# Score and value-query products of a recurrent attention as pairs of 64-row array tiles

## The chip, the cores and the metric

The kernel runs on one core of a Trainium2 chip. The metric is the device time of one execution in microseconds (us). The core has five engines with queues of their own: TensorE (PE, with its weight loads listed as PEld), VectorE (DVE), ScalarE (ACT), GpSimd (POOL) and SyncE (SP), which starts most of the transfers. An engine runs its queue in order and waits on semaphores for the others. PE writes its results to PSUM, which has eight banks of 128 partitions by 512 float32 words; DVE and ACT bring them back to the main on-chip memory.

## The reference

Three stages follow each other. The attention is a recurrence over 768 tokens for 4 batches of 8 heads with 40 dimensions; its output is the input of a mixture of 8 experts, and that of one a two-layer network.

```python
for t in range(S):
    y[:, :, t] = np.einsum('bhd,bhde->bhe', rt, state)
    Sa = np.einsum('bhde,bhe->bhd', state, at)
    state_decay = state * wt[:, :, None, :] - np.einsum('bhd,bhe->bhde', Sa, bt)
    state = state_decay + np.einsum('bhd,bhe->bhde', vt, kt)
...
logits = x @ w_gate                      # x: the attention's output, 3072 x 320
expert_idx = np.argmax(logits, axis=1)   # each token to one expert, in order, up to its capacity
h = np.maximum(np.einsum('ecd,edf->ecf', disp, w1), 0.0)
y = np.einsum('ecf,efd->ecd', h, w2)     # times the gate, back to the tokens' rows
...
h = x @ w_in
g = np.where(h > 0.0, h, alpha * (np.exp(np.minimum(h, 0.0)) - 1.0))
return (g @ w_out).astype(np.float32)
```

## The kernel before

**Units.** The attention is done in chunks of 64 tokens. A unit is one chunk of half the batches, 16 matrices for 16 pairs of batch and head; there are 24 units (12 chunks, two halves each), and a chunk needs the state that the chunk before it left. The 40 dimensions of a head lie on 64 partitions, two heads (called hp or x, 0 and 1) on partitions 0 to 63 and 64 to 127, so that most tiles are 128 partitions high with 8 groups (called q) along the row.

**Steps.** Each step is a generator, and each yield ends a part. `pre_dve(u)` (p) forms the running products of the decays by two scans on DVE (L220, L225), multiplies a by one (L230) and k and b by the other (L232). `pre_act(u)` (a) copies the scaled a on ACT into block-diagonal form (L241, tile `Abd`, off-diagonal blocks zero) and once more next to the masked scores (L243, tile `AM`). `scores(u, g)` (c) multiplies k and b against a for four of the eight groups (L254, tile `sc`); ACT copies the lower half of the result for the triangular inverses (L258), and `am_evac` (m) masks the upper half on DVE (L272). `q_mm(u, g)` (q) multiplies the solved values against the queries (L502, tile `q`, moving operand `Rbd`, block-diagonal as well) and masks the result on DVE (L507). Around them stand `kb_tr` (k, L281 and L283), `t64` (g, L410 and L421, preceded by a transpose on DVE, L403), `u_solve` (u, L446), `vu_tr` (w, L456), `s_update` (s, L471 on PE, L480 to L485 behind it), `s_tr` (h, L493), `y_state` and `y_mm` (z and y, L516 and L529, then L533 on DVE), `rhs` (r, L436) and `x_out` (x, L539, then L544 on ACT and L546 on DVE). GpSimd solves the triangles for four units at a time (L328, L330).

**Order.** The order of issue on every engine is fixed by the program: a table, `ORDER`, for the first five slots, and `slot(k)` for each later slot k. Slot k finishes unit k, and computes the scores of unit k + 8 and the scans of unit k + 9, as long as there are such units. In a slot from k = 5 to 15 the string that `slot` returns reads, in part (c.0 and c.1 stand for the score steps of unit k + 8, q.0 and q.1 for the value-query steps of unit k - 1; several marks of one name are its parts):

```
r r c.0 g g m.0 c.0 x x x g g (i) c.1 m.1 c.1 c.1 l q.0 q.0 u u q.1 q.1 h h (b) k.0 k.0 k.1 k.1 e p p p g w w w w a a z d t s s s y y
```

Slots 16 to 24 have the same without c, m, l, k, e, p and a. PSUM is one pool of seven banks that are handed out in turn (`bank`), and an eighth for y.

**After the attention** the experts and the second network run as blocks of 512 rows. They begin with rows that the attention has scattered to device memory (`disp`), so their first block can't start before the attention's last units are done.

Of the kernel before, what the change touches and what calls it, by code (L numbers as in the profile page):

```python
# [23 lines left out]
# units whose inverses start from blocks of 16 rows, and those with a plain product for the turn of k and b  # L24
FU, KMU = 4, 8
GROUPS = [(u, 2) for u in range(0, FU, 2)] + [(u, 4) for u in range(FU, NU, 4)]
# parts of the steps (see steps in attention) in the order of issue up to slot KR; slot() gives the later ones
KR = 5
ORDER = """
se1 sa0 se0 se0 v1 sc0 e0.0 sv se1 e0.1 sd p0 sw p0 e1.0 sw a0 p0 v0 p1 sa1 sx a0 p1 lw sz v2 st2 ss2 st1 e2.0 c0.0 a1  # L30
# [68 lines left out]
def attention(tc, nc, e_in, v_tok, d_in, wg, disp, cst, ring, early):  # L99
# [11 lines left out]
    # tiles that the first weights take over when the loads and scores are done  # L111
# [19 lines left out]
    Abd = [sh[2][:, 1024 * i:1024 * i + 1024].rearrange("p (x q t) -> p x q t", x=2, t=64) for i in range(2)]  # L131
# [28 lines left out]
    def set_a(i):  # L160
        nc.gpsimd.memset(Abd[i], 0.0)
# [55 lines left out]
    def pre_dve(u):  # L217
        e, s, g, d = EI[u % 2], SE[u % 2], GE[u % NGE], DF
        pc = PC[0:104, u % NPC, :]
        nc.vector.tensor_tensor_scan(  # L220
            out=s[0:104, ::-1], data0=e[0:104, 2:522][:, ::-1], data1=DR[0:104, ::-1],
            initial=0.0, op0=ALU.mult, op1=ALU.add)
        nc.vector.tensor_tensor(pc, s[0:104, 0:520:65], e[0:104, 1:521:65], op=ALU.mult)
        nc.vector.reciprocal(d[0:104, 0:520:65], pc)
        nc.vector.tensor_tensor_scan(  # L225
            out=g[0:104], data0=e[0:104, 0:520], data1=d[0:104],
            initial=0.0, op0=ALU.mult, op1=ALU.add)
        a, kb = Aes[u % 2][0:104].rearrange("p (q t) -> p q t", t=64), KBt[u % 2][0:104]
        yield
        nc.vector.tensor_tensor(a, a, q64(g)[0:104], op=ALU.mult)  # L230
        yield
        nc.vector.tensor_tensor(kb, kb, q64(s)[0:104].unsqueeze(2).to_broadcast([104, 8, 2, 64]), op=ALU.mult)  # L232

    def pre_act(u):
        AM, A = AMs[u % (LOOK + 1)], Abd[u % 2]
        for hp in range(2):
            if hp:
                yield
            r = slice(64 * hp, 64 * hp + 64)
            x = Aes[u % 2][r].rearrange("p (q t) -> p q t", t=64)  # L240
            nc.scalar.copy(A[r, hp], x)  # L241
            if u >= 2:
                nc.scalar.copy(AM[64:128, :, hp, :], x)  # L243

    # 64 x 64 matrices in rows of 4160: their diagonal blocks of 16 start 1040 apart
# [3 lines left out]
    def scores(u, g):  # L249
        A, kb = Abd[u % 2], KBt[u % 2]  # L250
        p = st["sc", u, g] = bank("sc")
        for i in range(4):
            q = 4 * g + i
            nc.tensor.matmul(  # L254
                p[:, 128 * i:128 * i + 128], kb[:, q].rearrange("p x t -> p (x t)"),
                A[:, :, q, :], start=True, stop=True)
        yield
        nc.scalar.copy(AB[64:128, :, 2 * g:2 * g + 2], p[64:128, :].rearrange("p (j b y) -> p b j y", j=2, b=2))  # L258
        if g == 0:
            return  # L260
# [9 lines left out]
    def am_evac(u, g):  # L270
        AM, p = AMs[u % (LOOK + 1)], st["sc", u, g]
        nc.vector.tensor_tensor(  # L272
            AM[0:64, 4 * g:4 * g + 4].rearrange("p q x t -> p (q x) t"), p[0:64, :].rearrange("p (l t) -> p l t", t=64),
# [15 lines left out]
    # inverses of triangles: of 16 rows for the first two pairs of units, of 32 for each four of the others  # L289
# [19 lines left out]
    def solve(g):  # L309
        """the inverse a part of its steps at a time"""  # L310
# [55 lines left out]
    # unit 1 has what a later unit's scores take over  # L366
# [3 lines left out]
    def t32(u):  # L370
        """blocks of 32 rows from those of 16"""
# [27 lines left out]
    def t64(u):  # L399
        """blocks of 64 rows from those of 32"""  # L400
# [86 lines left out]
    def s_tr(u):  # L487
        # for unit u: S0' in d-major
# [8 lines left out]
    def q_mm(u, g):  # L497
        V, R = VUt[u % 2], Rbd[u % 2]
        p = bank("q")
        for i in range(4):  # L500
            h = 4 * g + i
            nc.tensor.matmul(p[:, 128 * i:128 * i + 128], V[:, h].rearrange("p x t -> p (x t)"), R[:, h], start=True, stop=True)  # L502
# [3 lines left out]
        Qs, m = st["Qs", u], mask.unsqueeze(1).to_broadcast([128, 8, 64])  # L506
        nc.vector.tensor_tensor(Qs[:, 4 * g:4 * g + 4].rearrange("p h b t -> p (h b) t"), p.rearrange("p (l t) -> p l t", t=64), m, op=ALU.mult)  # L507
# [44 lines left out]
    def route(u, n=2):  # L552
        """expert of the tokens of n units from u on"""
# [14 lines left out]
    def route_mm(u, n=2):  # L568
        """their rows"""
# [38 lines left out]
    def go(key):  # L608
        """the next part of a step"""
# [31 lines left out]
def consts(p):  # L641
    """tiles that last, unset"""
# [29 lines left out]
def set_rest(nc, c):  # L672
# [3 lines left out]
    t = c["tri"]                          # 1 where k < m  # L676
    g.affine_select(out=t, in_=t, pattern=[[1, 128]], base=0, channel_multiplier=-1, compare_op=ALU.is_gt, fill=0.0)
    t = c["blk"]                          # same half
    g.memset(t[0:64, 64:128], 0.0)
    g.memset(t[64:128, 0:64], 0.0)  # L680
    t = c["tmo"]                          # same half: -1 where k >= m
# [3 lines left out]
    t = c["l1"]                           # first half before second half  # L685
# [11 lines left out]
class Ring:  # L697
    """tiles in turn, each for the weights of four tiles: [tile][three k tiles of stage one | stage two]"""
# [9 lines left out]
class Weights:  # L708
# [8 lines left out]
    def split(s, g):  # L717
        """high and low parts, a tile at a time"""
# [26 lines left out]
def ahead(W):  # L745
    """loads and splits of the first weights, a piece at a time"""
    W.fetch(0)
    yield
    yield from W.split(0)
    W.fetch(1)  # L750


def ffn(tc, nc, cst, disp, cap, w1, w2, w_in, w_out, out, ring, W0):
# [6 lines left out]
    # results: 512 rows of each expert, then a row of every token for those past them  # L760
# [6 lines left out]
    def convert():  # L767
        """float64 bits of the second network's weights to float32, rounded to nearest; a piece at a time"""
# [17 lines left out]
        for i, (g, k) in enumerate(jobs):  # L786
# [14 lines left out]
            # magnitudes below the least normal float32 become zero  # L801
# [9 lines left out]
    class Block:  # L811
        """512 rows through one pair of weights"""
# [17 lines left out]
        def start(s):  # L830
            """load and preparation of a block that nothing hides, a tile of rows at a time"""
# [68 lines left out]
    def elu(p, H, L):  # L900
        # GpSimd has the weights to split in the first block
# [6 lines left out]
        # exp(n) - 1 = (exp(n) + 1) tanh(n / 2), which keeps its digits at small n  # L908
# [5 lines left out]
    def gates():  # L914
        """gate weight of every token, zero where the expert is full"""
# [39 lines left out]
        # row of the result: inside the first 512 of its expert, or the token's own  # L955
# [14 lines left out]
    def run(blocks, extra, back=1):  # L970
        """blocks in turn; side work spread over the stages"""
# [22 lines left out]
    # experts  # L994
# [4 lines left out]
    def experts(r, dyn=False, more=None):  # L999
        Ws = [W0 if not dyn and e == 0 else expert(nc, ring, w1, w2, e) for e in range(8)]  # L1000
        hs = [(W, h) for W in Ws for h in range(2)] + ([] if dyn else [(W2, 0), (W2, 1)])
        def put(Y, i, dst, last):
            # the last rows on their own where the gathers wait for them
# [63 lines left out]
    def overflow():  # L1067
        # rows past the first 512 of an expert
# [24 lines left out]
        with tc.For_i(1, nr, 1) as r:  # L1093
            # zero rows behind the last row in use
# [11 lines left out]
            # this round's results to the tokens' own rows  # L1106
# [37 lines left out]
def host_layout(r, k, v, w, a, b):  # L1144
    def e_side(x):
        # [4, 8, 768, 40] -> [c, B2, hp, e, j, bp, t]
        y = x.reshape(2, 2, 4, 2, 12, 64, 40)          # B2 bp j hp c t e
# [3 lines left out]
    # decays with a zero before each chunk and two behind the last  # L1151
# [5 lines left out]
    y = v.reshape(2, 2, 4, 2, 12, 64, 40)              # B2 bp j hp c t d  # L1157
    v_tok = np.ascontiguousarray(y.transpose(4, 0, 5, 2, 1, 3, 6)).reshape(24, 64, 640)

    def d_side(x):  # L1160
        y = x.reshape(2, 2, 8, 12, 64, 40)             # B2 bp h c t d
# [39 lines left out]
```

## Time and profile before

| | us |
|---|---|
| median of 3 runs (1161.91, 1166.55, 1170.0) | 1166.55 |
| span of the profiled execution, first to last instruction | 1160.2 |
| PE busy in it | 1004.3 |
| DVE busy | 769.6 |
| POOL busy | 615.1 |
| ACT busy | 498.3 |

The profiled execution's span is 1.7 us below the fastest of the three timed runs and 6.35 us below their median. Its time stamps start at the first instruction. A float32 matmul stands in the profile as two records, each with a weight load of its own. The busy time of PE counts a matmul until its modelled end, while the next one has already begun, so starts of neighbouring rows tell more of its pace than lengths do.

### The profile page before, as it was taken

How to read it: one execution, taken by the hardware profiler on the slowest of the kernel's cores; microseconds unless marked ns; L12 is line 12 of the kernel's file. 1: busy time of each engine (PE TensorE's matmuls, PEld its weight loads, DVE VectorE, ACT ScalarE, POOL GpSimd, SP SyncE). 2: the span in 40 equal slices, each digit the busy share in tenths (PEclk: the TensorE clock that was granted, in tenths of full speed). 3: DMA queues.
4: the chain of work that ended last, by engine and by line, in shares of the span. 5: the costliest groups of instructions: out<-in, count | busy, mean ns of one | idle time of the engine just before them, and what ended most of it. 6: DMA issues, size and time to landing. Idle time of an engine off the chain costs nothing. (4 is left out here: it accounts for less than half of the span.)

```text
span 1160.2 us, 25498 instructions
## 1 busy us (share of the span) xinstructions
PE 1004.3 (87%) x10287; PEld 910.5 (78%) x10287; DVE 769.6 (66%) x1234; ACT 498.3 (43%) x968; POOL 615.1 (53%) x699
## 2 busy tenths in 40 slices
PE   5777889888899995788977798969999999999992
PEld 5777888788799894777867687847799999999992
DVE  8767666766765343588977888948666666666652
ACT  4555455545454341232332233325555455545441
POOL 4759577684928522345544545626664545454451
PEclk8878888988889897898988998979999999999997
DMA  6687764667644444425465646413010101010001
GB/s 173 160 177 200 180 139 101 129 167 168 150 116 101 130 116 142 142 80 190 149 179 176 193 131 201 173 57 123 1 46 1 46 1 46 1 46 1 23 1 29
DMA packets 189214, 127.25 MB, mean 110 GB/s; under 512 B 102776, under 2 KB 177016, under 8 KB 187448
## 3 DMA queue, kind: packets, MB, share of 16 engines
q1 hardware_dynamic: 185336, 108.65, 35.8%
q0 software_dynamic: 3168, 11.03, 2.9%
q10 hardware_dynamic: 576, 5.77, 1.3%
q8 instruction: 85, 1.39, 0.5%
q14 instruction: 49, 0.40, 0.1%
HBM read 87.39 MB, written 38.03 MB: 108 GB/s over the span
## 5 line engine op out<-in xcount | busy, mean ns | idle before, releaser
L912 POOL TENSOR_TENSOR L<-E,H 128x512 fp32r<-128x512 f32 x91 | 141.8, 1558 | 162.7 <-ACT H L911 157.4
L885 PE MATMUL po<-ring,L 128*128 128x320 f32 x640 | 200.8, 314 | 14.0 <-DVE L L898 9.9
L883 PE MATMUL po<-ring,H 128*128 128x320 f32 x640 | 199.0, 311 | 1.3 <-ACT H L911 0.8
L723 POOL TENSOR_TENSOR ring<-ring,ring 128x704 fp32r<-128x704 f32 x80 | 147.3, 1853 | 98.1 <-ACT ring L722 83.8
L884 PE MATMUL po<-ring,H 128*128 128x320 f32 x640 | 198.5, 310 | 0.0
L869 PE MATMUL ph<-XH,ring 128*128 128x512 f32 x640 | 185.6, 413 | 4.6 <-DVE XL L860 4.0
L885 PEld LDWEIGHTS po<-ring,L 128*128 128x128 f32 x640 | 121.1, 189 | 18.7 <-DVE L L898 12.4
L869 PEld LDWEIGHTS ph<-XH,ring 128*128 128x128 f32 x640 | 117.6, 196 | 22.7 <-DVE XL L860 5.0
L883 PEld LDWEIGHTS po<-ring,H 128*128 128x128 f32 x640 | 121.5, 190 | 10.5 <-ACT H L911 4.4
L884 PEld LDWEIGHTS po<-ring,H 128*128 128x128 f32 x640 | 121.1, 189 | 6.0
L905 ACT ACTIVATE E<-N 128x512 f32<-128x512 f32 x96 | 60.8, 633 | 150.3 <-POOL L L912 115.6
L904 DVE TENSOR_SCALAR N<-ph 128x512 f32<-128x512 f32 x96 | 66.0, 688 | 74.9 <-PE ph L869 74.7
L330 POOL TENSOR_TENSOR X<-X,ring 128x60 f32<-128x60 f32 (+19 forms) x170 | 105.7, 622 | 13.3
L254 PE MATMUL sc<-ring,ring 128*128 128x128 f32 x384 | 70.5, 346 | 36.9 <-ACT ring L241 25.5
L869 PE MATMUL ph<-XL,ring 128*128 128x512 f32 x320 | 101.8, 400 | 0.0
L869 PE MATMUL ph<-XS,ring 128*128 128x512 f32 x320 | 100.9, 397 | 0.0
L254 PEld LDWEIGHTS sc<-ring,ring 128*128 128x128 f32 x384 | 62.7, 250 | 39.3 <-ACT ring L241 29.6
L328 POOL TENSOR_TENSOR ring<-X,ring 128x60 f32<-128x60 f32 (+19 forms) x108 | 63.4, 587 | 55.9 <-DMA ring<-dab 34.3
L909 DVE SCALAR_TENSOR_TENSOR M<-E,M 128x512 f32<-128x512 f32 x96 | 81.3, 846 | 2.5 <-ACT M L906 2.5
L797 POOL TENSOR_TENSOR M<-M,N 128x320 f32<-128x320 f32 (+1 forms) x28 | 29.5, 1053 | 89.4 <-DVE M L795 89.4
L843 PE MATMUL pt<-ident,X 128*128 128x128 f32 (+1 forms) x168 | 30.8, 314 | 49.9 <-DMA X<-disp 41.4
L869 PEld LDWEIGHTS ph<-XL,ring 128*128 128x128 f32 x320 | 62.3, 195 | 14.7
(212 smaller groups left out, 1997.5 us busy)
## 6 DMA issues: line engine op xcount, KB each, us to landing
ring<-in_w_dram SPq DMA_DIRECT2D x16, 640.0 KB
ring<-in_e_in_dram SPq DMA_DIRECT2D x28, 321.6 KB
ring<-in_w_dram SPq DMA_DIRECT2D x32, 256.0 KB
RVU<-in_d_in_dram SPq DMA_DIRECT2D x48, 160.0 KB
dab<-AB SPq DMA_DIRECT2D x24, 256.0 KB
ring<-w ACTq DMA_DIRECT2D x4, 1408.0 KB
disp<-ring SPq DMA_DIRECT2D x8, 640.0 KB
S<-in_w_out_dram SPq DMA_DIRECT2D x16, 320.0 KB
```

Source lines behind the costliest of these rows:

```text
L254: nc.tensor.matmul(p[:, 128 * i:128 * i + 128], kb[:, q].rearrange("p x t -> p (x t)"), A[:, :, q, :], start=True, stop=True)
L328: nc.gpsimd.tensor_tensor(tv, X[:, 0:n, s:s + 1].to_broadcast([128, n, m]), N[:, s:s + 1, s + 1:e].to_broadcast([128, n, m]), op=ALU.mult)
L330: nc.gpsimd.tensor_tensor(X[:, 0:n, s + 1:e], X[:, 0:n, s + 1:e], tv, op=ALU.subtract)
L723: s.nc.gpsimd.tensor_tensor(s.L[g][:, c], R[:, c], s.H[g][:, c].bitcast(F32), op=ALU.subtract)
L869: nc.tensor.matmul(p, l, r, start=i == 0, stop=i == len(seq) - 1)
L883: nc.tensor.matmul(o, H[:, c], hb, start=f == 0, stop=False)
L884: nc.tensor.matmul(o, H[:, c], lb, start=False, stop=False)
L885: nc.tensor.matmul(o, L[:, c], hb, start=False, stop=last)
L904: nc.vector.tensor_scalar(N, p, 0.0, None, op0=ALU.min)
L905: nc.scalar.activation(out=E, in_=N, func=AF.Exp)
L909: nc.vector.scalar_tensor_tensor(out=M, in0=E, scalar=1.0, in1=M, op0=ALU.add, op1=ALU.mult)
L912: eng.tensor_tensor(L, E, H.bitcast(F32), op=ALU.subtract)
```

## The change

The off-diagonal zeros are no longer multiplied. The two heads of a group, on partitions 0 to 63 and 64 to 127, get a matmul each, with 64 rows of contraction, the same 128 weight columns, and 64 moving columns instead of 128; the first writes to one PSUM bank, the second to another. A group of eight products is now sixteen, and all sixteen are issued by the first part of the first step (c.0, q.0); the second step (c.1, q.1) only evacuates the second bank. Evacuations keep their number and size; their index says which head, no longer which four groups.

`Abd` and its copies on ACT (L241) are gone: DVE writes the scaled a to a tile of its own (`As`, three in turn), from which PE reads directly and ACT makes the copy next to the scores. The zeros that `Abd` needed at the start (two memsets of 128 x 1024 on POOL) become one of 32 x 1536. `Rbd` stays as it is, since `y_state` uses it; `q_mm` takes its diagonal blocks. The rest of the diff strips comments.

```diff
-se1 sa0 se0 se0 v1 sc0 e0.0 sv se1 e0.1 sd p0 sw p0 e1.0 sw a0 p0 v0 p1 sa1 sx a0 p1 lw sz v2 st2 ss2 st1 e2.0 c0.0 a1
+se1 sa se0 se0 v1 sc0 e0.0 sv se1 e0.1 sd p0 sw p0 e1.0 sw a0 p0 v0 p1 sx a0 p1 lw sz v2 st2 ss2 st1 e2.0 c0.0 a1
...
-    Abd = [sh[2][:, 1024 * i:1024 * i + 1024].rearrange("p (x q t) -> p x q t", x=2, t=64) for i in range(2)]
+    As = [sh[2][:, 512 * i:512 * i + 512].rearrange("p (q t) -> p q t", t=64) for i in range(3)]
...
-    def set_a(i):
-        nc.gpsimd.memset(Abd[i], 0.0)
+    def set_a():
+        nc.gpsimd.memset(sh[2][96:128, 0:1536], 0.0)
...
-        nc.vector.tensor_tensor(a, a, q64(g)[0:104], op=ALU.mult)
+        nc.vector.tensor_tensor(As[u % 3][0:104], a, q64(g)[0:104], op=ALU.mult)
...
     def pre_act(u):
-        AM, A = AMs[u % (LOOK + 1)], Abd[u % 2]
+        AM = AMs[u % (LOOK + 1)]
         for hp in range(2):
             if hp:
                 yield
-            r = slice(64 * hp, 64 * hp + 64)
-            x = Aes[u % 2][r].rearrange("p (q t) -> p q t", t=64)
-            nc.scalar.copy(A[r, hp], x)
             if u >= 2:
-                nc.scalar.copy(AM[64:128, :, hp, :], x)
+                nc.scalar.copy(AM[64:128, :, hp, :], As[u % 3][64 * hp:64 * hp + 64])
...
-    def scores(u, g):
-        A, kb = Abd[u % 2], KBt[u % 2]
-        p = st["sc", u, g] = bank("sc")
-        for i in range(4):
-            q = 4 * g + i
-            nc.tensor.matmul(
-                p[:, 128 * i:128 * i + 128], kb[:, q].rearrange("p x t -> p (x t)"),
-                A[:, :, q, :], start=True, stop=True)
-        yield
-        nc.scalar.copy(AB[64:128, :, 2 * g:2 * g + 2], p[64:128, :].rearrange("p (j b y) -> p b j y", j=2, b=2))
-        if g == 0:
+    def scores(u, hp):
+
+        if ("sc", u) not in st:
+            kb, a = KBt[u % 2], As[u % 3]
+            st["sc", u] = P = [bank("sc") for _ in range(2)]
+            for q in range(8):
+                for x in range(2):
+                    r = slice(64 * x, 64 * x + 64)
+                    nc.tensor.matmul(P[x][:, 64 * q:64 * q + 64], kb[r, q].rearrange("p x t -> p (x t)"), a[r, q], start=True, stop=True)
+        yield
+        p = st["sc", u][hp]
+        nc.scalar.copy(AB[64:128, :, :, 64 * hp:64 * hp + 64], p[64:128, :].rearrange("p (j b t) -> p b j t", b=2, t=64))
+        if hp == 0:
             return
...
-    def am_evac(u, g):
-        AM, p = AMs[u % (LOOK + 1)], st["sc", u, g]
+    def am_evac(u, hp):
+        AM, p = AMs[u % (LOOK + 1)], st["sc", u][hp]
         nc.vector.tensor_tensor(
-            AM[0:64, 4 * g:4 * g + 4].rearrange("p q x t -> p (q x) t"), p[0:64, :].rearrange("p (l t) -> p l t", t=64),
+            AM[0:64, :, hp, :], p[0:64, :].rearrange("p (q t) -> p q t", t=64),
             mask[0:64].unsqueeze(1).to_broadcast([64, 8, 64]), op=ALU.mult)
...
-    def q_mm(u, g):
-        V, R = VUt[u % 2], Rbd[u % 2]
-        p = bank("q")
-        for i in range(4):
-            h = 4 * g + i
-            nc.tensor.matmul(p[:, 128 * i:128 * i + 128], V[:, h].rearrange("p x t -> p (x t)"), R[:, h], start=True, stop=True)
+    def q_mm(u, b):
+        if ("q", u) not in st:
+            V, R = VUt[u % 2], Rbd[u % 2]
+            st["q", u] = P = [bank("q") for _ in range(2)]
+            for h in range(8):
+                for bp in range(2):
+                    r = slice(64 * bp, 64 * bp + 64)
+                    nc.tensor.matmul(P[bp][:, 64 * h:64 * h + 64], V[r, h].rearrange("p x t -> p (x t)"), R[r, h, bp], start=True, stop=True)
         yield
...
-        Qs, m = st["Qs", u], mask.unsqueeze(1).to_broadcast([128, 8, 64])
-        nc.vector.tensor_tensor(Qs[:, 4 * g:4 * g + 4].rearrange("p h b t -> p (h b) t"), p.rearrange("p (l t) -> p l t", t=64), m, op=ALU.mult)
+        nc.vector.tensor_tensor(
+            st["Qs", u][:, :, b, :], st["q", u][b].rearrange("p (h t) -> p h t", t=64),
+            mask.unsqueeze(1).to_broadcast([128, 8, 64]), op=ALU.mult)
```

On PE in slot 8, from the last `rhs` to the first `kb_tr`, the kernel before issues these matmuls (a row is the line, the tile written, the operands, the shape of one result and the number of matmuls; `sc` holds scores, `xp` and `t` the two products of `t64`, `q` the value-query products, `ut` those of `u_solve`):

```order
L436 MATMUL rhs<-VS_146,AM_143 64x40 x16
L254 MATMUL sc<-ring_99,ring_97 128x128 x4
L410 MATMUL xp<-AB,TA 32x32 x16
L539 MATMUL x<-IW,XT 128x88 x4
L421 MATMUL t_2882<-TT_129,TA 32x32 x16
L254 MATMUL sc<-ring_99,ring_97 128x128 x4
L502 MATMUL q<-RVU_126 128x128 x4
L446 MATMUL ut<-TT_129,RH_130 64x64 x16
L502 MATMUL q<-RVU_126 128x128 x4
L493 MATMUL s<-ident,S0E_132 128x104 x4
```

In the changed kernel the same place reads:

```order
L435 MATMUL rhs<-VS_146,AM_143 64x40 x16
L254 MATMUL sc<-ring_99,ring_97 128x64 x16
L409 MATMUL xp<-AB,TA 32x32 x16
L541 MATMUL x<-IW,XT 128x88 x4
L420 MATMUL t_3044<-TT_129,TA 32x32 x16
L503 MATMUL q<-RVU_126 128x64 x16
L445 MATMUL ut<-TT_129,RH_130 64x64 x16
L492 MATMUL s<-ident,S0E_132 128x104 x4
```

The second half of the scores has moved ahead of both products of `t64` and of `x`, and the second half of the value-query products ahead of `u_solve`.

On ACT in the same slot, from `vu_tr` to the copy of `x_out`, the kernel before issues (`ring_99` is the shared buffer that holds `Abd`, `ring_98` the one with the loaded operands):

```order
L460 COPY VU<-vu 128x320 x2
L241 COPY ring_99<-ring_98 64x512
L243 COPY AM_143<-ring_98 64x8x64
L241 COPY ring_99<-ring_98 64x512
L243 COPY AM_143<-ring_98 64x8x64
L485 COPY VS_145<-S0E_133 64x8x40
L438 COPY RH_131<-rhs 128x320
L415 COPY TA<-xp 32x256 x2
L258 COPY AB<-sc 64x2x256
L544 COPY XO<-x 128x320
```

And the changed kernel (`ring_99` now holds `As`):

```order
L459 COPY VU<-vu 128x320 x2
L240 COPY AM_143<-ring_99 64x8x64 x2
L484 COPY VS_145<-S0E_133 64x8x40
L437 COPY RH_131<-rhs 128x320
L414 COPY TA<-xp 32x256 x2
L257 COPY AB<-sc 64x8x64
L546 COPY XO<-x 128x320
```

The two copies into `Abd` are gone, and nothing else has moved. DVE issues the same instructions in the same order in both kernels.

## Rows read from the trace of the kernel before

**Rows 1.** Busy time by stretch: length, PE, PEld, DVE, ACT, POOL, PEclk, DMA.

```profile
11.00:151.00 140.00, 113.43 (x1908) 107.63 (x1910) 99.03 (x154) 74.77 (x158) 85.29 (x170) 0.81 0.74 180
151.00:343.00 192.00, 169.77 (x2959) 159.20 (x2956) 129.26 (x229) 95.89 (x210) 131.59 (x201) 0.86 0.59 140
343.00:434.00 91.00, 88.69 (x1925) 83.15 (x1925) 40.87 (x104) 38.04 (x91) 48.09 (x75) 0.94 0.47 111
434.00:1160.20 726.20, 632.41 (x3505) 560.54 (x3501) 492.11 (x720) 285.97 (x501) 340.22 (x227) 0.94 0.28 88
```

**Rows 2.** Waits from 151 to 343 us: total, times, longest.

```profile
DVE Qs L507 <- PE q L502: 23.8, 22, 2.0
...
PE sc L254 <- ACT ring L241: 14.5, 9, 3.5
```

**Rows 3.** Timeline of DVE in slot 8: start, length, instruction, idle before it.

```profile
206.18 1.22 DVE L232 TENSOR_TENSOR ring<-ring 104x1024 f32<-104x1024 f32 x1
...
209.56 0.69 DVE L533 TENSOR_TENSOR XT<-y,GE 104x512 f32<-104x512 f32 x1
...
214.07 0.69 DVE L507 TENSOR_TENSOR Qs<-q,mask 128x512 f32<-128x512 f32 x1 [0.21 <-PE q L502]
216.24 0.69 DVE L507 TENSOR_TENSOR Qs<-q,mask 128x512 f32<-128x512 f32 x1 [1.48 <-PE q L502]
216.85 1.23 DVE L220 TENSOR_TENSOR_SCAN ring<-ring,DR 104x520 f32<-104x520 f32 x1
```

**Rows 4.** Timeline of PE in slot 8.

```profile
208.24 1.16 PE L254 MATMUL sc<-ring,ring 128*128 128x128 f32 x8 [1.53 <-ACT ring L241]
...
210.31 1.12 PE L539 MATMUL x<-IW,XT 128*128 128x88 f32 x8 [0.29 <-DVE XT L533]
211.36 0.69 PE L421 MATMUL t<-TT,TA 32*32 32x32 f32 x32
211.99 1.16 PE L254 MATMUL sc<-ring,ring 128*128 128x128 f32 x8
212.98 1.06 PE L502 MATMUL q<-RVU 128*128 128x128 f32 x8
213.97 1.15 PE L446 MATMUL ut<-TT,RH 64*64 64x64 f32 x32
215.05 1.16 PE L502 MATMUL q<-RVU 128*128 128x128 f32 x8
216.04 0.52 PE L493 MATMUL s<-ident,S0E 104*128 104x104 f32 x4
```

**Rows 5.** Timeline of the weight loads in slot 8 (rows*columns of the weights).

```profile
204.34 1.02 PEld L529 LDWEIGHTS y<-Qs,KB 128*64 128x64 f32 x32
...
210.31 0.97 PEld L539 LDWEIGHTS x<-IW,XT 128*128 128x128 f32 x8 [0.40 <-DVE XT L533]
...
212.87 0.97 PEld L502 LDWEIGHTS q<-RVU 128*128 128x128 f32 x8
213.97 1.01 PEld L446 LDWEIGHTS ut<-TT,RH 64*64 64x64 f32 x32
```

**Rows 6.** Timeline of ACT in slot 8.

```profile
206.30 0.62 ACT L241 COPY ring<-ring 64x512 f32<-64x512 f32 x1 [3.19 <-DVE ring L230]
...
207.57 0.61 ACT L241 COPY ring<-ring 64x512 f32<-64x512 f32 x1
```

**Rows 7.** Groups of the whole span: busy, mean ns, idle before and its releasers.

```profile
L241 ACT COPY ring<-ring 64x512 f32<-64x512 f32 x48 | 29.6, 617 | 46.4 <-DVE ring L230 42.1 <-POOL TOK L692 3.6
```

**Rows 8.** Timeline of PE in slot 10, at the lower clock.

```profile
244.54 2.08 PE L254 MATMUL sc<-ring,ring 128*128 128x128 f32 x8 [3.51 <-ACT ring L241]
```

**Rows 9.** Timeline of DVE in slot 10.

```profile
242.49 1.65 DVE L232 TENSOR_TENSOR ring<-ring 104x1024 f32<-104x1024 f32 x1
...
256.28 0.69 DVE L507 TENSOR_TENSOR Qs<-q,mask 128x512 f32<-128x512 f32 x1 [1.47 <-PE q L502]
```

## The prediction

> **What bounds the kernel now.** I read the busy times by stretch first. The products that change stand before 434 us; from there on the experts and the second network run [rows 1], which the change doesn't touch and which begin with rows that the attention has written. So a microsecond saved before 434 us is one saved at the end, and the question is what sets the pace there. There are three stretches. Up to 151 us the program fills its pipeline (13 score steps, 4 value-query steps), with PE busy 113.43 of 140 us. From 151 to 343 us run slots 5 to 15, eleven slots of 17.5 us, each with one score step and one value-query step; PE is busy 169.77 of 192 us and DVE 129.26. From 343 us no scores are left, and PE is busy 88.69 of 91 us: it is the bound there, back to back.
>
> For the middle stretch, the waits show DVE and PE waiting for each other: the mask of the value-query products (L507) waits 23.8 us for PE, and the scores (L254) 14.5 us for the ACT copies into `Abd` [rows 2]. The timelines of slot 8 show the loop. DVE ends the scaling of k and b at 207.40 [rows 3]; PE starts the scores at 208.24, behind the second `Abd` copy, which ran from 207.57 to 208.18 [rows 4, 6]; `x` begins at 210.31, held by DVE's L533, which ends at 210.25 [rows 3, 4]; then come the second scores, the first q, `u_solve` and the second q at 215.05, and DVE, after its first L507, stands still for 1.48 us until the second [rows 3, 4]. Behind that second L507 the scans of the next unit (L220, 216.85) are queued, and with them the next slot. That is what a change has to shorten.
>
> **The matmuls themselves.** Four products of 128 x 128 by 128 columns take 0.99 us, from 211.99 to the next group at 212.98 and again to 213.97 [rows 4], so a step of eight takes 1.98. What sets this? The eight weight loads of `x` last 0.97 us and those of q last 0.97 too [rows 5], though `x` streams 88 columns and q 128. So the load of 128 weight columns sets the pace, 0.12 us each, and not the moving columns, which are all that the change halves. Per step there are now 32 loads of 128 columns, where there were 16.
>
> Rows matter as little: 32 loads of 64 columns take 1.01 us in `u_solve` with 64 rows and 1.02 in `y_mm` with 128 [rows 5]. The Trainium skill, TensorE: Matmul & The Clock Gate, section LDWEIGHTS, states it as a rule that speaks against this change: a load's time goes by columns, and a load with few rows takes as long as one with all. The rows above agree, though none of them shows a load of 64 rows by 128 columns. By that rule alone, loads one behind the other, a step would take 3.9 us; it is the second case below.
>
> But two array tiles can load at once: 32 loads of 64 columns are 2048 columns in 1.01 us, against 1024 in 0.97 for q [rows 5]. In `u_solve` the two tiles differ in rows and in columns, in `y_mm` in columns alone; no row has tiles that differ in rows alone, as here. So the price of a step lies between 0.97 us (the pair side by side and the 64 moving columns as the measure) and 32 x 0.12 = 3.9 us (no overlap at all). I take the pair side by side with 128 columns as the measure, 16 x 0.12 = 1.94 us, which is nearest to the rows of `u_solve`: PE's time stays as it was. (The Trainium skill, TensorEngine Tiling, section Key Properties, says that different tiles can load and multiply in parallel; the trace agrees for the tiles it has.)
>
> **What moves.** Taking slot 8 with steps of 1.95 us. The scores wait for `As` and for the scaled k and b, so they start at 207.45 instead of 208.24 and end at 209.4; the first half of `t64` takes 0.65 and `x` still waits for L533 until 210.31, so the 0.8 us are lost there. The second `t64` starts at 211.36 as now, and PE goes straight to q at 211.99 and ends it at 213.94. The first L507 starts at 214.1, as now (214.07). The second no longer waits behind `u_solve`: it follows after 0.61, at 214.7, and L220 at 215.3 instead of 216.85. Gain 1.55 us, all of it from closing the gap of 1.48 before the second L507.
>
> In slots at half clock, such as slot 10 (2.08 us for the same eight records [rows 8]), PE is the bound from the scores to q, and its work is the same. There the gain is the earlier start, 244.54 minus the end of L232 at 244.14 [rows 8, 9], 0.4 us, plus the 1.08 of `u_solve` that no longer lie ahead of the second L507 (which waits 1.47 in that slot too [rows 9]), less the 0.61 of the first: 0.87. A mean granted clock of 0.86 [rows 1] between levels of 1 and 0.5 means 28% of the stretch at half clock, 3 slots of 11. Sum for the middle: 8 x 1.55 + 3 x 0.87 = 15.0 us.
>
> Before 151 us: ACT loses 26 of the 48 copies of 0.617 us [rows 7], 16 us, but it is busy 74.77 of 140 us [rows 1], and where PE waited for a copy there, k and b were ready little earlier; between 0 and half of the 16, I take 2. The memsets on POOL (two of 128 x 1024 against one of 32 x 1536) lie beside loads that the first scan waits for: nothing. After 343 us: same loads, same number of mode changes around q (`t64`, q, `u_solve`, `s_tr`), nothing. Two PSUM banks are held at once instead of one after the other; the seven banks go round in about half a slot, and the bank that comes seven allocations after the scores is that of `u_solve`, behind both of their evacuations, so no wait is added. Evacuations move the same number of words with a stride of 64 words inside the row; I count nothing. What hides the longer first score group (1.95 instead of 1.0 us before `t64`) is DVE's work up to L533; without it each slot would lose 0.8.
>
> Sum: 15 + 2 = 17 us off the span of 1160.2, which gives 1143.2. The median of the timed runs is 6.35 us over that span, so 1149.6: **1150 us**.
>
> **The rivals.**
> - *PE gives it back* (no change). If PE is the bound in most of the middle slots, not DVE's chain, closing DVE's gap only lengthens another wait. For it: PE is busy 88% of that stretch. Against: it still waits 14.5 us for the copies and 1.53 us in slot 8 [rows 2, 4]. Gain per slot 0.4 us: 1166.55 - 11 x 0.4 = 1162.
> - *The loads of the two row tiles queue* (slower). A step takes 3.96 instead of 1.98 us. In slot 8: scores to 211.4, `x` 212.05, second `t64` 213.1, q from 213.75 to 217.7, the two masks, L220 at 219.2: 2.35 us later than now. Times 11 slots 26 us; 9 value-query steps after 343 us, where PE has no slack, 18; 17 steps before 151 us at 1.98, about 27 of 34 since PE is busy 81%. Sum 71 minus 2: 1235 us. It decides if the loads of a pair overlap by less than about a fifth. For it: no row shows two loads into the same columns at once. Against: both kinds of pairs that the trace has do overlap.
> - *Half the columns, half the time* (much faster). A step takes 0.97. The slots at half clock, bound by PE, gain about 3 us more each, the last 9 value-query steps 1 each, the 17 early ones half of that: 17 + 9 + 9 + 8.5 = 43, so 1123 us. Against it stand the equal loads of `x` and q. The Trainium skill, TensorEngine Tiling, section Theoretical Speedup, has this rule: up to 2x for a small contraction. The rows on loads disagree, as long as a tile still takes 128 weight columns.
>
> **How the numbers follow.** Chances: forecast 0.50, PE gives it back 0.25, loads queue 0.20, half the time 0.05. The range takes in the first two, with the whole of the early 16 us and part of PE's 14.5 us of waits below the forecast (1128), and a partial overlap of the loads above (up to 1205): about 0.8. Runs of this kernel differ by 0.7%, so 1% (11.7 us, below 1154.9) is about what can be told from no change. Faster 0.50 (0.46 of the forecast's 0.50, and the last rival, rounded), same 0.28, slower 0.22.
>
> **What would show it.** Right: pairs of score records that start within a few ns of each other, a step still 1.8 to 2 us from its first start to the next group; no wait before the second L507; slots 5 to 15 shorter by about 1.4 us; ACT's 48 copies gone; nothing changed after the attention's end except its start. Wrong: a score step of 3 to 4 us on PE, or of 1 us; or the gap before L507 closed and a new one of the same size before L533, L546 or the scores. A mean clock in the middle stretch that falls below 0.86 would cost PE what the chain gains.

## The result, and where the time went

The changed kernel takes 1177.06 us (median of five runs, 1171.93 to 1182.96) against 1166.55 (1161.91 to 1170.0, five runs): 1.0104 times as long, 95% interval 1.0072 to 1.0135. It is slower by 1%, where 1.4% faster was forecast. Its profiled execution spans 1175.1 us, 14.9 more than that of before. The medians differ by 10.5: the profile of the kernel before lies 6.35 us below its median, that of the changed kernel 2.0.

One instruction marks the progress of the attention in every kernel here: the scaling of the state product on DVE (tile `XT`, L533 before, L535 after), once per unit. These are its third, 14th and last start, first before, then after (start, length, instruction, idle before it).

```profile
135.97 0.69 DVE L533 TENSOR_TENSOR XT<-y,GE 104x512 f32<-104x512 f32 x1 [1.28 <-PE y L529]
...
335.54 0.69 DVE L533 TENSOR_TENSOR XT<-y,GE 104x512 f32<-104x512 f32 x1
...
441.70 0.69 DVE L533 TENSOR_TENSOR XT<-y,GE 104x512 f32<-104x512 f32 x1 [0.32 <-PE y L529]
```

```profile
167.95 0.69 DVE L535 TENSOR_TENSOR XT<-y,GE 104x512 f32<-104x512 f32 x1 [6.35 <-PE y L531]
...
349.58 0.69 DVE L535 TENSOR_TENSOR XT<-y,GE 104x512 f32<-104x512 f32 x1
...
460.02 0.69 DVE L535 TENSOR_TENSOR XT<-y,GE 104x512 f32<-104x512 f32 x1 [0.59 <-PE y L531]
```

They cut the span into four stretches. The start-up takes 168.0 us instead of 136.0 (+32.0), the eleven slots with scores 181.6 instead of 199.6 (-18.0), the last slots 110.4 instead of 106.2 (+4.2), and everything after the attention 715.1 instead of 718.5 (-3.4). The sum is +14.8, the 14.9 of the spans. So the slots gain more than was forecast, and the start-up takes it all away and more.

What PE did there is in its busy times by the same stretches (columns as in [rows 1]), first before the change, then after it.

```profile
11.00:136.00 125.00, 101.83 (x1724) 96.78 (x1726) 90.59 (x141) 69.55 (x147) 81.14 (x162) 0.82 0.74 185
136.00:335.50 199.50, 174.16 (x3020) 163.27 (x3018) 134.08 (x235) 96.47 (x210) 135.74 (x209) 0.84 0.62 143
335.50:441.70 106.20, 102.91 (x2180) 96.33 (x2173) 50.15 (x137) 43.11 (x102) 50.03 (x77) 0.95 0.45 106
```

```profile
11.00:168.00 157.00, 153.48 (x2021) 144.07 (x2021) 90.06 (x142) 55.90 (x123) 82.08 (x165) 1.00 0.64 154
168.00:350.00 182.00, 171.73 (x3310) 162.47 (x3309) 134.51 (x236) 83.66 (x189) 136.20 (x203) 0.84 0.61 144
350.00:460.00 110.00, 107.08 (x2352) 99.39 (x2350) 48.82 (x136) 42.54 (x101) 54.12 (x82) 0.92 0.48 114
460.00:1175.10 715.10, 625.18 (x3383) 554.05 (x3383) 485.87 (x694) 285.50 (x500) 339.18 (x225) 0.94 0.29 88
```

In the start-up PE is busy 153.48 of 157 us; it was 101.83 of 125. The granted clock reads 1.00 there, but that is no full clock: the trace has no record of the clock before 166.6 us, and the column has nothing to average. The lengths of rows tell the level. This is PE's timeline of the start-up before the change:

```profile
11.00 3.76 PE L254 MATMUL sc<-ring,ring 128*128 128x128 f32 x16 [11.00 <-ACT ring L241]
14.57 1.95 PE L281 MATMUL kbt<-ident,ring 104*128 104x104 f32 x16
```

And after it, at the beginning and at the end of the start-up:

```profile
11.18 3.68 PE L254 MATMUL sc<-ring,ring 64*128 64x64 f32 x32 [11.18 <-DVE ring L232]
14.79 3.74 PE L280 MATMUL kbt<-ident,ring 104*128 104x104 f32 x16
...
134.20 3.68 PE L254 MATMUL sc<-ring,ring 64*128 64x64 f32 x32
137.81 2.01 PE L541 MATMUL x<-IW,XT 128*128 128x88 f32 x8
...
169.28 1.12 PE L541 MATMUL x<-IW,XT 128*128 128x88 f32 x8
```

Both kernels do their first scores at the lower clock, 1.2 GHz. Before, the clock rose at 14.6 us, behind sixteen records of 128 rows and 128 moving columns, and the sixteen records of the first transposes took 1.95 us. After, the same transposes take 3.74 us. `x` takes 2.01 us at 137.81 and 1.12 at 169.28 (1.12 in [rows 4]): from 11 to 166 us PE works at 1.2 GHz, almost without a pause.

In the eleven slots the granted clock is 0.84 in both kernels, and the gain is PE's idle time: 10.3 us of 182 after, 25.3 of 199.5 before. Slot 7 of the changed kernel, at the upper clock, on PE, then on DVE:

```profile
218.08 2.00 PE L254 MATMUL sc<-ring,ring 64*128 64x64 f32 x32
220.01 0.69 PE L409 MATMUL xp<-AB,TA 32*32 32x32 f32 x32
...
222.68 2.00 PE L503 MATMUL q<-RVU 64*128 64x64 f32 x32
224.62 1.15 PE L445 MATMUL ut<-TT,RH 64*64 64x64 f32 x32
```

```profile
224.87 1.29 DVE L507 TENSOR_TENSOR Qs<-q,mask 128x512 f32<-128x512 f32 x2 [0.99 <-PE q L503]
...
227.19 1.24 DVE L220 TENSOR_TENSOR_SCAN ring<-ring,DR 104x520 f32<-104x520 f32 x1
```

A score step takes 1.93 us from its start to the next group, a value-query step 1.94, and the two masks follow each other (`x2` in one row) where [rows 3], slot 8 of the kernel before, has 1.48 us between them.

### The profile page after: what moved, and what is told of

Read it like the earlier page. It is cut to its first block, busy times and chain, and to the rows that moved or that the text cites. A ratio compares the mean times of both kernels' runs of the same rounds, so it can differ in the third digit from the quotient of the medians.

```text
span 1175.1 us, 26971 instructions
## 1 busy us (share of the span) xinstructions
PE 1057.5 (90%) x11055; PEld 960.0 (82%) x11055; DVE 767.3 (65%) x1234; ACT 470.0 (40%) x920; POOL 621.4 (53%) x698
## 5 line engine op out<-in xcount | busy, mean ns | idle before, releaser
L885 PEld LDWEIGHTS po<-ring,H 128*128 128x128 f32 x640 | 121.2, 189 | 10.2 <-ACT H L913 4.2
L327 POOL TENSOR_TENSOR ring<-X,ring 128x60 f32<-128x60 f32 (+19 forms) x108 | 68.6, 635 | 45.1 <-DMA ring<-dab 24.8
L254 PE MATMUL sc<-ring,ring 64*128 64x64 f32 x768 | 73.0, 360 | 18.8 <-DVE ring L232 12.3
L254 PEld LDWEIGHTS sc<-ring,ring 64*128 64x128 f32 x768 | 69.0, 269 | 21.8 <-DVE ring L232 12.5
L871 PEld LDWEIGHTS ph<-XS,ring 128*128 128x128 f32 x320 | 61.6, 192 | 14.0
```

The lines of the kernel that those rows point to most:

```text
L254: nc.tensor.matmul(P[x][:, 64 * q:64 * q + 64], kb[r, q].rearrange("p x t -> p (x t)"), a[r, q], start=True, stop=True)
L327: nc.gpsimd.tensor_tensor(tv, X[:, 0:n, s:s + 1].to_broadcast([128, n, m]), N[:, s:s + 1, s + 1:e].to_broadcast([128, n, m]), op=ALU.mult)
L871: nc.tensor.matmul(p, l, r, start=i == 0, stop=i == len(seq) - 1)
L885: nc.tensor.matmul(o, H[:, c], hb, start=f == 0, stop=False)
```

## The experiments

Theory: the narrow score products keep TensorE at its lower clock in the start-up, and the slots gain by the order of issue. The table has all kernels. The first column is the first record of the upper clock, the next four are the stretches between the marks above (all from one profiled execution each), then the median and the ratio to the kernel before run beside it, all in us.

| kernel | clock first up at | start-up | eleven slots | last slots | rest | median | ratio, 95% interval |
|---|---|---|---|---|---|---|---|
| before | 14.6 | 136.0 | 199.6 | 106.2 | 718.5 | 1166.55 | |
| after | 166.6 | 168.0 | 181.6 | 110.4 | 715.1 | 1177.06 | 1.0104 (1.0072 to 1.0135) |
| e1 score pairs alone | 95.4 | 147.2 | 200.0 | 104.7 | 716.7 | 1167.37 | 1.0017 (0.9979 to 1.0055) |
| e2 value-query pairs alone | 15.8 | 143.4 | 188.4 | 111.5 | 713.7 | 1160.81 | 0.9966 (0.9927 to 1.0005) |
| e3 after, 128 columns | 15.1 | 145.0 | 181.9 | 110.7 | 715.9 | 1158.17 | 0.9981 (0.9947 to 1.0015) |
| e4 before, q ahead | 16.2 | 138.1 | 188.6 | 110.4 | 717.3 | 1158.01 | 0.9949 (0.9916 to 0.9982) |
| e5 q ahead in slots 5 to 15 | 15.4 | 142.1 | 186.5 | 111.0 | 717.8 | 1157.09 | 0.9940 (0.9912 to 0.9967) |
| e6 e5, all scores first | 15.4 | 136.7 | 188.8 | 113.9 | 717.4 | 1157.11 | 0.9939 (0.9908 to 0.9971) |
| e7 after, early products | 7.9 | 162.1 | 181.3 | 115.1 | 712.1 | 1167.97 | 1.0049 (1.0010 to 1.0089) |
| e8 after, tiles in a row | 136.6 | 207.2 | 220.9 | 136.7 | 713.5 | 1283.28 | 1.1023 (1.0971 to 1.1075) |
| e9 e3 in the start-up alone | 23.8 | 140.1 | 182.5 | 115.1 | 717.9 | 1158.13 | 0.9940 (0.9906 to 0.9973) |
| e10 e3 with the copies | 14.3 | 141.6 | 187.3 | 112.3 | 718.9 | 1157.45 | 0.9943 (0.9906 to 0.9979) |
| e11 e3, step t later | 23.6 | 138.8 | 181.5 | 106.6 | 718.5 | 1150.15 | 0.9898 (0.9820 to 0.9977) |
| e12 e5, step t later | 17.3 | 138.9 | 193.2 | 104.5 | 712.6 | 1155.69 | 0.9921 (0.9892 to 0.9951) |

How much one profile can differ from another shows in the start-ups of before, e4, e5 and e6 (136.0 to 142.1, nearly the same code) and in the slots of e5 and e12 (186.5 and 193.2, the same work but for the place of some loads).

**e1, scores alone.** `q_mm` is that of the kernel before, all else as changed.

```diff
-                    nc.tensor.matmul(P[bp][:, 64 * h:64 * h + 64], V[r, h]..., R[r, h, bp], ...)
+            nc.tensor.matmul(p[:, 128 * i:128 * i + 128], V[:, h]..., R[:, h], ...)
```

> The scores as pairs of row tiles, the value-query products as in the kernel before. Theory A (in the start-up the narrow score products leave TensorE at its lower clock): no rise of the granted clock in the first 100 us, eight loads of the first transposes 0.21 us apart as in the changed kernel, and a time of 1170 to 1190 us, at or above the changed kernel's 1177. Rival B (the lower clock in that one profile has another cause, the value-query pairs or the moved steps): the clock rises at about 15 us as in the kernel before, and the time is 1155 to 1167 us.

The clock came up at 95.4 us and the time is 1167.37 us: below the range of theory A, at the edge of B's, though the start-up is A's. PE's timeline around the rise shows what ran.

```profile
14.67 3.74 PE L280 MATMUL kbt<-ident,ring 104*128 104x104 f32 x16
...
88.82 3.68 PE L254 MATMUL sc<-ring,ring 64*128 64x64 f32 x32
92.43 0.96 PE L455 MATMUL vu<-ident,RVU 104*128 104x104 f32 x4
93.18 3.04 PE L501 MATMUL q<-RVU 128*128 128x128 f32 x16
96.06 0.52 PE L455 MATMUL vu<-ident,RVU 104*128 104x104 f32 x4
```

The first transposes take 3.74 us, as in the changed kernel. The first value-query products, 128 x 128 by 128 columns here, begin at 93.18 us, and in the middle of them the clock rises: the same four transposes take 0.96 us ahead of them and 0.52 behind. The slots gain nothing (200.0): score pairs without the copies bring nothing here, where the second mask waits behind the solve.

**e2, value-query products alone.** The kernel before with the changed `q_mm`.

```diff
-            nc.tensor.matmul(p[:, 128 * i:128 * i + 128], V[:, h]..., R[:, h], ...)
+                    nc.tensor.matmul(P[bp][:, 64 * h:64 * h + 64], V[r, h]..., R[r, h, bp], ...)
```

> The value-query products as pairs of row tiles, all ahead of the solve, the scores as in the kernel before. Theory A: the clock rises at about 15 us as before, the start-up takes as long as before, and slots 5 to 15 give the 12 us that they gave in the changed kernel: 1150 to 1158 us. Rival B (value-query pairs cost the clock): no early rise, 1170 us or more. Rival C (the gain of the slots came from the scores and the copies that are gone): early rise, but 1163 to 1168 us.

The clock rises early, as theory A has it, and the slots gain 11 us, close to the 12 that it names; the median, 1160.81, stays 3 us above its range.

**e3, wider score products.** The changed kernel with one edit:

```diff
-  nc.tensor.matmul(P[x][:, 64 * q:64 * q + 64], kb[r, q]..., a[r, q], ...)
+  n = 128 if q < 7 else 64
+  nc.tensor.matmul(P[x][:, 64 * q:64 * q + n], kb[r, q]..., a[r]...[:, 64 * q:64 * q + n], ...)
```

> The changed kernel with 128 moving columns in the score products in place of 64 (the second 64 are those of the next head; the next product writes over their results). Same loads, same tiles, twice the columns streamed. Theory A1 (what the narrow products lack is streamed columns): the clock rises within the first 20 us, score steps stay near 1.8 us at the upper clock since loads set their pace, and the time is 1150 to 1160 us. Theory A2 (what they lack is rows, two tiles of 64 rows do not count like one of 128): no rise in the first 100 us, 1175 to 1185 us. If streamed columns set the pace of two tiles, a step at the upper clock takes over 2.5 us.

PE's timeline of the start-up, and of slot 9:

```profile
10.90 3.68 PE L255 MATMUL sc<-ring,ring 64*128 64x128 f32 x32 [10.90 <-DVE ring L232]
14.51 2.29 PE L281 MATMUL kbt<-ident,ring 104*128 104x104 f32 x16
...
228.00 2.00 PE L255 MATMUL sc<-ring,ring 64*128 64x128 f32 x32
229.93 0.69 PE L410 MATMUL xp<-AB,TA 32*32 32x32 f32 x32
```

Twice the moving columns cost PE nothing: 3.61 us per step at the lower clock, as before the edit, and 1.93 at the upper. But the clock rises at 15.1 us, the start-up takes 145.0 us instead of 168.0, and the ratio to the kernel before, 0.9981, lies clear of the changed kernel's 1.0104. Theory A1 holds in this start-up: the same row tiles with 128 moving columns got the early rise. The start-up is still a little above the 136.0 to 143.4 us of the kernels with block-diagonal scores; here the clock was down again from 18.5 to 42.4 us.

**e4, order alone.** The kernel before, with the second half of the value-query products ahead of the solve.

```diff
-    if k > 1: a(f"q{k-1}.0 q{k-1}.0")
+    if k > 1: a(f"q{k-1}.0 q{k-1}.1 q{k-1}.0")
...
-    if k > 1: a(f"q{k-1}.1 q{k-1}.1")
+    if k > 1: a(f"q{k-1}.1")
```

> The kernel before with one edit in the order of a slot: both halves of the value-query products (128 x 128, block-diagonal) are issued ahead of the solve's products, from slot 2 on. No pairs, copies as before. If the gain of slots 5 to 15 is that the second mask no longer waits behind the solve's products: the second L507 follows the first without the 1.48 us gap, 8 to 16 us in all, 1150 to 1158 us, with the clock's first rise at about 15 us. If the order gave nothing: 1163 to 1170 us.

1158.01 us, at the upper edge of the first case: 11.0 us less in the eleven slots, and no start-up lost. Most of what the change gains in the slots needs no pairs.

**e5, that order in slots 5 to 15.** As e4, but only `if ups`.

```diff
+    if k > 1: a(f"q{k-1}.0 q{k-1}.1 q{k-1}.0" if ups else f"q{k-1}.0 q{k-1}.0")
...
+    if k > 1: a(f"q{k-1}.1" if ups else f"q{k-1}.1 q{k-1}.1")
```

> As e4, but the value-query products go ahead of the solve only in slots 5 to 15; slots 16 to 24 keep the order of the kernel before. The profile of e4 gained 11 us in the slots with scores and gave some 4 us back in the slots without them. If that loss is the solve being held up where PE is the bound: slots 16 to 24 take as long as in the kernel before (about 106 us from the 14th to the last scaling of the state product by DVE, against 110 in e4), and 1151 to 1157 us. If the 4 us were chance (the clock): no difference from e4, 1158.

A miss: the last slots take 111.0 us with the old order, as with the new. So the order of those slots does not cost the 4 us given back there; PE is idle for 8.7 us of them, against 3.3 in the kernel before (e11).

**e6, the change's order with block-diagonal products.** e5, and `scores` issues all eight products at its first call:

```diff
-        for i in range(4):
-            q = 4 * g + i
+        if ("sc", u, g) not in st:
...
+            for q in range(8):
```

> The order of the changed kernel without its pairs: the 128 x 128 block-diagonal products, Abd and its copies stay, but all eight score products of a unit are issued by the first score step, and in slots 5 to 15 all eight value-query products ahead of the solve. If the gain of slots 5 to 15 comes from the order and from the first scores not waiting for halves: those slots gain 11 to 18 us as in the changed kernel, with the clock rising at about 15 us: 1147 to 1156 us. If the pairs themselves (or the copies that are gone) make the part beyond e4's 11 us: 11 us or less, 1154 to 1160 us.

188.8 us in the slots, 10.8 less than before, no better than e5: moving the scores gives nothing by itself.

**e7, early products.** The changed kernel with fourteen 128 x 128 products on PE while it waits for its first operands.

```diff
+        for i in range(n):
+            nc.tensor.matmul(p[:, 0:128], ident, ident, start=True, stop=True)
```

> The changed kernel with 14 products of 128 x 128 by 128 columns (unit matrix times itself, into a bank that nobody reads) on PE from about 5 us on, while it waits for the first operands. Theory A1 (narrow score products don't keep the upper clock in the start-up either): the clock rises at 8 to 11 us and is back at the lower level within 25 us, the start-up takes nearly as long as in the changed kernel, 1170 to 1178 us. Rival (it takes only one opening, the rest of the work holds it): the upper clock for about half of the start-up as in the kernel before, 1155 to 1164 us.

PE's timeline of the start-up:

```profile
4.76 4.87 PE L197 MATMUL warm<-ident 128*128 128x128 f32 x28 [4.76 <-POOL ident masks.py:199]
11.08 2.00 PE L259 MATMUL sc<-ring,ring 64*128 64x64 f32 x32 [1.45 <-DVE ring L237]
13.01 2.03 PE L285 MATMUL kbt<-ident,ring 104*128 104x104 f32 x16
19.50 3.68 PE L259 MATMUL sc<-ring,ring 64*128 64x64 f32 x32 [4.46 <-DVE ring L237]
23.11 3.74 PE L285 MATMUL kbt<-ident,ring 104*128 104x104 f32 x16
```

The clock is up from 7.9 to 18.1 us, and the first scores take 1.93 us. Ahead of the second scores PE stands still for 4.46 us; they run at the lower clock, and it stays low until 110.3 us: one opening doesn't last. The start-up takes 162.1 us. The median, 1167.97, is 2 us below the range of A1.

**e8, tiles in a row.** The changed kernel with the two loops of `scores` and of `q_mm` exchanged: eight products on rows 0 to 63, then eight on rows 64 to 127.

```diff
-            for q in range(8):
-                for x in range(2):
+            for x in range(2):
+                for q in range(8):
```

> The changed kernel with the sixteen products of a step in another order: the eight on rows 0 to 63, then the eight on rows 64 to 127, so that neighbours use the same tile. If the pace of 0.11 us for two loads comes from neighbours on different row tiles: a step takes 3.5 us or more at the upper clock and 7 at the lower (1.75 and 3.5 in pairs), and the kernel 1235 us or more. If loads overlap whatever the tile, because the next weights are loaded behind the running product: steps as in the changed kernel, about 1177 us.

PE's timeline at the upper clock:

```profile
385.81 3.39 PE L254 MATMUL sc<-ring,ring 64*128 64x64 f32 x32
389.13 1.02 PE L409 MATMUL xp<-AB,TA 32*32 32x32 f32 x32
```

3.32 us for the same 32 records that take 1.93 in pairs (the expectation had 3.5 or more), and 1283.28 us in all. The pace of the pairs comes from neighbours on different rows. The Trainium skill, TensorE: Matmul & The Clock Gate, section The mechanism, says that a weight load overlaps running products only when it goes to other rows. The worth of the order here is in line with that, but these rows don't tell loads from products; and [rows 5], where eight loads to all rows last 0.97 us beside 88 moving columns as beside 128, do not look as if each load waited for the product before it.

**e9, wider in the start-up alone.** e3 with the width bound to the units of the start-up.

```diff
-                    n = 128 if q < 7 else 64
+                    n = 128 if q < 7 and u < 13 else 64
```

> The changed kernel with 128 moving columns (e3's way) in the score products of units 0 to 12 alone, which is the start-up; units 13 to 23 keep 64. If the changed kernel lost its time only in the start-up: the clock rises at about 15 us, the third scaling of the state product by DVE stands near 145 us as in e3 (168 in the changed kernel), the eleven slots after it take about 182 us as in both, and the time is 1153 to 1163 us. If the narrow products cost the clock in the slots as well: the slots take over 186 us, 1163 us or more.

The start-up takes 140.1 us and the slots, with 64 columns, 182.5: the narrow scores cost the changed kernel time in the start-up and not in the slots. 1158.13 us, as expected; the clock came up at 23.8 us rather than 15.

**e10, the copies back.** e3, with PE reading a copy of `As` that ACT makes in two halves.

```diff
+            nc.scalar.copy(Ac[u % 2][64 * hp:64 * hp + 64], As[u % 2][64 * hp:64 * hp + 64])
...
-            kb, a = KBt[u % 2], As[u % 3]
+            kb, a = KBt[u % 2], Ac[u % 2]
```

> e3 with the two copies on ACT back: As is copied half by half to another tile of the same form, and PE reads the copy (two copies of 64 x 512 per unit, as into Abd before). e3 gained 18 us in the eleven slots, the order alone (e4 to e6) 11 to 13. If the rest comes from the copies that no longer stand between DVE and the scores: the slots take 187 us or more here (182 in e3), 1160 us or more. If it comes from the row tiles or their evacuations: 182 us, about 1158.

The slots take 187.3 us, as with the block-diagonal products in their new order (186.5 to 188.8 in e4 to e6). The five kernels without copies and with q ahead (after, e3, e7, e9, e11) lie at 181.3 to 182.5. The six with copies and q ahead (e2, e4, e5, e6, e10, e12) lie at 186.5 to 193.2. So the copies are worth some 5 us of the 18 in this stretch, and the row tiles nothing that shows. In the timed runs the copies cost nothing that shows: the ratio is 0.9943 with them and 0.9981 without (e3), the intervals overlap, and the 1160 us expected for this case did not come. Where the 5 us go is not shown.

**e11, step t later.** e3, with the loads of the solved triangles moved behind the loads for the solver.

```diff
+    if nx < NU: a(f"t{nx}")
...
-    if k + 2 < NU: a(f"t{k+2}")
```

> e3 with the loads of the solved triangles (step t) moved from the end of a slot to behind the next slot's loads for the solver (step l), one unit later at the same place in time. In e3 SP stood 8.0 us at these loads in slot 14, waiting for GpSimd's solve, with the last unit's scores queued behind, and GpSimd started its last group 13 us after those scores, 6.7 us in the kernel before. If that wait is what the last slots give back: the last group starts 5 to 8 us earlier and the kernel takes 1149 to 1155 us. If the loads come too late for the slots at their new place: 1160 us or more.

One cause of what the last slots lose shows here. SP, which starts the transfers, waits in e3 from 320 to 350 us (waits: total, times, longest; then the timelines of ACT, SP and POOL):

```profile
SPq L356 <- DMA dx<-X: 8.0, 1, 8.0
```

```profile
331.88 0.58 ACT L258 COPY AB<-sc 64x512 f32<-64x512 f32 x1 [0.24 <-DVE AM L272]
...
334.37 0.32 SPq L356 DMA_DIRECT2D TA<-dx  x1
...
339.06 0.54 SPq L268 DMA_DIRECT2D dab<-AB  x1
...
345.43 0.23 POOL L328 TENSOR_TENSOR ring<-X,ring 128x31 f32<-128x31 f32 x1 [7.61 <-DMA ring<-dab]
```

The last scores are ready at 332.46 us, but their transfer (L268) stands behind loads (L356) that wait for GpSimd's previous solve; GpSimd starts its last group at 345.43, 13 us behind the scores. The same in e11:

```profile
323.58 0.58 ACT L258 COPY AB<-sc 64x512 f32<-64x512 f32 x1
...
324.19 0.50 SPq L268 DMA_DIRECT2D dab<-AB  x1
...
331.70 0.23 POOL L328 TENSOR_TENSOR ring<-X,ring 128x31 f32<-128x31 f32 x1 [8.83 <-DMA ring<-dab]
```

The transfer starts with the scores, the solve 7.5 us behind them, the last slots take 106.6 us instead of 110.7, and the kernel 1150.15: the fastest median here, below both kernels (four runs, 1145.62 to 1160.79; the interval of its ratio overlaps e3's a little).

**e12, the same on e5.** The loads move as in e11:

```diff
+    if nx < NU: a(f"t{nx}")
...
-    if k + 2 < NU: a(f"t{k+2}")
```

> e5 (block-diagonal products, value-query products ahead of the solve in slots 5 to 15) with the same move of step t as e11. SP waited there for GpSimd's solve as well (last group 10.8 us behind the last scores). Expected 3 to 5 us below e5 if the wait counts: 1150 to 1155 us; 1157 if it doesn't.

1155.69 us, 1.4 below e5 and 0.7 above the range. The last slots gain 6.5 us (104.5 against 111.0), but the eleven slots take 193.2 us in this profile. The loads at their later place are not what lengthens them: PE is idle there for 22.7 us (24.0 in e5) and busy for 170.47 instead of 162.54, at a granted clock of 0.86 instead of 0.91.

## Why the prediction was wrong

**The step that failed** is the start-up's term, "between 0 and half of the 16, I take 2", and under it "PE's time stays as it was". It priced each product at the clock that the kernel before had been granted, and took that clock for a property of the place in the program. Here it went with the products themselves: behind sixteen records with 128 moving columns it rose at 14.6 us, with the narrow ones it stayed low until 166.6. The term was -2 us; it measured +32.0. e3 and e9 show the cause, since they change only the width of the score products and bring the start-up back to 145.0 and 140.1 us; e1 shows the rise in the first wide group. The prediction named a falling clock as what could go wrong, but for the middle stretch, and gave it no price. None of the rivals was this one.

**The price of a step** was right: 1.95 us forecast, 1.93 and 1.94 measured, with the pair side by side and 128 weight columns as the measure. So the rival of queueing loads did not come true; e8 shows that it does when neighbours share their rows, at 3.32 us (3.96 in the rival). The rival of half the time falls as well.

**The gain in the slots** was right in kind and a little small: 18.0 us for a forecast of 15.0. The gap ahead of the second mask closed, and 11 to 13 us of the gain come from that order alone (e4, e5, e6; 6.4 in e12, at its lower clock). The 0.8 us by which the scores start earlier, which I called lost at `x`, are not lost as far as one profile each can tell: 5.4 us over eleven slots, by e10 against e3. That PE would give it back did not happen.

**The last slots** were put at nothing and lost 4.2 us. In the changed kernel that is PE's busy time at a lower granted clock, not a wait: PE is busy 107.08 of 110 us at 0.92, before 102.91 of 106.2 at 0.95. Busy time times clock gives 98.5 and 97.8 us, nearly the same work (an estimate from these rows). Why the clock was lower was not tested; in the last slots of all kernels here but e8 it is 0.91 to 0.95 with value-query pairs and 0.93 to 0.98 with block-diagonal ones. SP's queue, where earlier scores meet a solve that comes no earlier, is the cause that e11 shows for e3, where PE is idle for 6.7 us. The changed kernel has that wait too (SP stands 4.0 us at the same loads, and the last group starts 10.2 us behind the last scores, against 6.7 in the kernel before), but PE is idle for only 2.9 us there, against 3.3 before.

**After the attention** nothing was forecast, and 3.4 us less were measured, with no experiment on it; the same stretch varies from 712.1 to 718.9 us over all kernels here.

Together: -2 became +32.0, -15.0 became -18.0, and +4.2 and -3.4 came on top, so that a forecast of -17 ended at +14.8 of the span, and at +10.5 between the medians.

## What to carry to other kernels

A change that makes products narrower can change the clock at which everything around them runs, as it did in this start-up; look at what ran before the clock rose in such a stage, and price the stage at both levels. Here 64 more columns in each product, which cost PE no time, were worth 14 us by the ratios (1.0104 against 0.9981) and 19 by the medians. And before a gain is put down to a new form of instruction, try the order that came with it alone: it gave most of the gain in the slots, and the rest of that stretch's gain went with copies that were no longer needed.

## What was not expected of the hardware

PE was busy for 153.48 of 157 us and stayed at 1.2 GHz until 166.6, with the products of this start-up (64 x 128 tiles with 64 columns, transposes of 104 columns, tiles of 32 and 64). In the middle of fourteen 128 x 128 products the clock rose, for 10.2 us; after a pause of 4.46 us the narrow work ran at the lower level until 110.3 us. Two row tiles of 64 rows took 128 moving columns each in the same 1.93 us per step as 64, so moving columns did not set that pace; that the loads of 128 weight columns do is the reading that fits it and the equal loads of [rows 5].
